# Projections as a stream of row-tile pairs, one-chunk score visits and AV by two pairs of heads, in a fused attention and feed-forward kernel

## Chip, cores, metric

One core of one Trainium2 chip. The metric is the device time of one execution in microseconds (us), the median of several runs. The clock granted to TensorE was full (1.00, or 0.99 over a whole run) throughout. A span from a profile is about 2 us shorter than the time of the same execution (466.3 against 468.6); spans are compared with spans and times with times.

## The reference

```python
scores = q @ k.T / sqrt(64)                      # 8 batches, 12 heads, 448 tokens, head size 64
attn   = maximum(scores, 0) ** 2 / 448
x      = (attn @ v), heads side by side          # 3584 tokens x 768
xn     = x / sqrt(mean(x * x) + 1e-6) * rms_g
out    = (silu(xn @ w_gate) * (xn @ w_val)) @ w_out    # 768 -> 1536 -> 768
```

## The kernel before

The feed-forward of batch b runs on TensorE while the attention of batch b+1 is slipped in between as "units". Only batch 0's attention runs alone. `merge` spreads the units over the feed-forward's groups.

Three things matter here. First, the shape of the matmuls. Each projection is issued as two halves of 64 output columns (column tiles, 128x64), which run side by side in the array. The norm's sums have the same shape, and AV's tiles (112x64) are column tiles too. Scores have only 64 rows to contract (the head size) and run as two row tiles (64x128). Second, the PSUM: 3 banks for projections, 4 for scores, 1 for AV. Third, the order of visits: per pair of heads j, two score visits of two chunks each; the second is followed by AV of the pair before.

```python
    def scores(b, j, cs):                       # cs = (0, 1) or (2, 3)
        for c in cs:
            psS = ps_s.tile([P, 2, 512], FP32, name="psS", tag="psS")
            for hh in range(2):                 # two row tiles, 64x128
                nc.tensor.matmul(out=psS[:, hh, :S], lhsT=qkT[...][:, c * PC : c * PC + P], rhs=qkT[...], ...)
        ...                                     # relu on ACT or DVE, square on DVE one visit later
    def attend(b, j):                           # AV of one pair of heads: 8 matmuls 112x64
        psAV = ps_a.tile([P, S], FP32, name="psAV", tag="ps_a")
        ...
    def project(b, *groups):
        for kt in range(KT):
            for ps, (w_sb, fb) in zip(pss, groups):
                for h in range(0, P, D):        # two column tiles, 128x64
                    nc.tensor.matmul(out=ps[h : h + D, :], lhsT=w_sb[:, kt, fb * P + h : fb * P + h + D],
                                     rhs=xns[b][:, kt, :], start=(kt == 0), stop=(kt == KT - 1))
    def outproj(i, t, o, w):                    # w = 512, then 256
        ...                                     # same two column tiles, 12 steps
    def attention(b):
        for j in range(HP):
            add(0.5, lambda j=j: scores(b, j, (0, 1)))
            ...
            add(1.2, lambda j=j: scores(b, j, (2, 3)), lambda j=j: j and attend(b, j - 1))
        ...
```

## Time and profile before

| | before |
|---|---|
| time, median | 468.63 us |
| span of the profiled run | 466.3 us |
| TensorE (PE) busy | 97% |
| DVE, ACT busy | 61%, 54% |
| chain that ended last, share of PE | 91% |

The first lines are from the page of the profiled run of the kernel before: busy us, share of the span and instructions of each engine, then the chain of work that ended last.

```profile
PE 454.5 (97%) x4768; PEld 257.6 (55%) x4768; DVE 283.6 (61%) x449; ACT 252.5 (54%) x380; POOL 55.8 (12%) x48
...
PE 91%; DVE 3%; ACT 2%; DMA 1%; issue 1%; POOL 0%; ACTq 0%; DVEq 0%; POOLq 0%
```

So TensorE sets the time. But busy does not say full: the ends of matmuls are modelled and they overlap. The groups of PE's matmuls by form show shapes and the mean length of one (the figure after the comma, in ns):

```profile
L302 PE MATMUL psP<-xn,wv_sb 128*64 128x448 bf16 x1152 | 126.9, 353 | 0.3 <-ACT sil L312 0.3
...
L339 PE MATMUL psO<-wo_sb,hT 128*64 128x512 bf16 x672 | 77.5, 379 | 0.0
L201 PE MATMUL psS<-qkT 64*128 64x448 bf16 x384 | 54.0, 354 | 3.3 <-ACT r L215 2.6 <-DVE qkT L179 0.7
...
L339 PE MATMUL psO<-wo_sb,hT 128*64 128x256 bf16 x672 | 41.8, 273 | 0.0
```

`128*64` and `64*128` are the tiles: column tiles and row tiles. The last column is idle time just before the group. It is next to nothing but for 3.3 us before the scores, nearly all of it in batch 0's attention, which runs alone; so PE hardly waits for anybody. Where the time goes is only seen in the starts. The timeline of PE in one stretch (start us, length us, what, how many):

```profile
205.66 0.92 PE L302 MATMUL psP<-xn,wg_sb 128*64 128x448 bf16 x8
206.51 0.55 PE L201 MATMUL psS<-qkT 64*128 64x448 bf16 x4
207.00 1.32 PE L302 MATMUL psP<-xn,wv_sb 128*64 128x448 bf16 x12
208.15 1.30 PE L302 MATMUL psP<-xn,wg_sb 128*64 128x448 bf16 x12
```

From 207.00 to 208.15 one group of six pairs takes 1.15 us, or 189 ns a pair (its first pair is 24 ns longer). The score visit starts at 206.51 and ends at 207.00: 0.49 us for two pairs that take 0.38 in a stream. The single starts of the trace show the rest: 285 ns pass from the last projection pair to the first score pair and 279 to 283 ns from the last score pair back, where 189 would do. These are the changes between column and row tiles. The Trainium skill ("TensorEngine Tiling (Array Packing)", Key Properties) says that changing the tiling mode drains TensorE; the trace agrees, with about 95 ns each way.

### The profile page before, as it was taken

The numbers are of one execution on the slowest core, as the hardware profiler recorded it, in microseconds if no ns is written. First come the engines' busy times: TensorE is split into PE (matmuls) and PEld (weight loads), VectorE is DVE, ScalarE is ACT, GpSimd is POOL, SyncE is SP. The second block draws the span as 40 slices with busy tenths as digits, with TensorE's granted clock in tenths as the row PEclk, the third lists the DMA queues.
The fourth block names the chain that finished last, engine by engine and source line by source line (L and its number), as shares of the span: only waits on it lengthen the run. The fifth ranks groups of instructions, "written<-read, shape, count | busy, mean of one in ns | idle before, by whom it ended". The sixth has DMA issues, their size and how long they took to land.

```text
span 466.3 us, 10899 instructions
## 1 busy us (share of the span) xinstructions
PE 454.5 (97%) x4768; PEld 257.6 (55%) x4768; DVE 283.6 (61%) x449; ACT 252.5 (54%) x380; POOL 55.8 (12%) x48
## 2 busy tenths in 40 slices
PE   7989999999999999999999999999999999999995
PEld 3336654655456445655456554565456554577774
DVE  2876497757745677557665578457773677562210
ACT  4872476566545666546645666546665566452221
POOL 8463000421012000400004000000000000000000
PEclk9999999999999999999999999999999999999999
DMA  9999999999919920499009940086001300021013
GB/s 113 200 204 200 209 168 129 116 208 158 82 33 173 201 29 1 53 214 135 1 2 143 211 83 1 7 173 103 1 2 38 100 2 1 0 70 34 1 37 101
DMA packets 128047, 43.56 MB, mean 93 GB/s; under 512 B 100608, under 2 KB 124416, under 8 KB 128000
## 3 DMA queue, kind: packets, MB, share of 16 engines
q0 software_dynamic: 88944, 23.60, 52.0%
q1 hardware_dynamic: 39056, 19.28, 20.9%
q8 instruction: 37, 0.61, 0.5%
q14 instruction: 10, 0.08, 0.1%
HBM read 47.19 MB, written 11.01 MB: 125 GB/s over the span
## 4 chain that ended last, share of the span: by engine, by line
PE 91%; DVE 3%; ACT 2%; DMA 1%; issue 1%; POOL 0%; ACTq 0%; DVEq 0%; POOLq 0%
PE psP L302 48%; PE psO L339 23%; PE psS L201 9%; PE psAV L230 8%; DVE r L218 2%; PE psB L139 1%; PE psSS L276 1%; DMA kb<-in_k_dram 1%; ACT r L215 1%; DVE r L213 1%; PE psT L174 1%; ACT xT L241 1%; DVE x L243 0%; POOL qb L93 0%; POOL kb L93 0%
## 5 line engine op out<-in xcount | busy, mean ns | idle before, releaser
L215 ACT ACTIVATE r<-psS 112x896 bf16<-112x896 f32 x147 | 128.4, 915 | 28.6 <-PE psS L201 28.4
L302 PE MATMUL psP<-xn,wv_sb 128*64 128x448 bf16 x1152 | 126.9, 353 | 0.3 <-ACT sil L312 0.3
L302 PE MATMUL psP<-xn,wg_sb 128*64 128x448 bf16 x1152 | 126.8, 353 | 0.0
L339 PE MATMUL psO<-wo_sb,hT 128*64 128x512 bf16 (+1 forms) x1344 | 112.5, 326 | 0.0
L317 DVE TENSOR_TENSOR hT<-sil,psP 128x448 bf16<-128x448 bf16 x96 | 59.6, 621 | 84.7 <-PE psP L302 82.6
L218 DVE TENSOR_TENSOR r<-r 112x896 bf16<-112x896 bf16 x189 | 109.9, 626 | 0.2 <-ACT r L215 0.2
L312 ACT ACTIVATE sil<-psP 128x448 bf16<-128x448 f32 x96 | 52.2, 545 | 97.2 <-PE psP L302 97.1
L339 PEld LDWEIGHTS <-hT 128*64 128x64 bf16 x1344 | 78.9, 110 | 31.7 <-issue 0.4
L302 PEld LDWEIGHTS <-wg_sb 128*64 128x64 bf16 x1152 | 66.4, 110 | 45.4 <-issue 7.4
L302 PEld LDWEIGHTS <-wv_sb 128*64 128x64 bf16 x1152 | 65.5, 110 | 46.7 <-issue 10.5
L346 ACT COPY ost<-psO 128x512 f32<-128x512 f32 (+1 forms) x56 | 26.7, 478 | 73.1 <-PE psO L339 73.1
L213 DVE TENSOR_SCALAR r<-psS 112x896 bf16<-112x896 f32 x45 | 49.0, 1089 | 27.6 <-PE psS L201 27.6
L201 PE MATMUL psS<-qkT 64*128 64x448 bf16 x384 | 54.0, 354 | 3.3 <-ACT r L215 2.6
L230 PE MATMUL psAV<-r,vb 112*64 112x448 bf16 x384 | 46.1, 358 | 1.0 <-DVE r L218 1.0
L285 DVE RECIPROCAL rstd<-rstd 128x448 f32<-128x448 f32 x8 | 23.6, 2953 | 19.9 <-ACT rstd L281 19.9
L201 PEld LDWEIGHTS <-qkT 64*128 64x128 bf16 x384 | 11.9, 94 | 37.7 <-issue 33.1
L230 PEld LDWEIGHTS <-vb 112*64 112x64 bf16 x384 | 18.4, 109 | 24.0 <-issue 15.3
L243 DVE TENSOR_TENSOR x<-xT 128x448 bf16<-128x448 bf16 x48 | 18.5, 385 | 20.7 <-ACT xT L241 20.7
L241 ACT ACTIVATE xT<-psAV 128x448 bf16<-128x448 f32 x48 | 26.2, 545 | 8.2 <-PE psAV L230 6.6
L93 POOL DMA_DIRECT2D vb<-in_v_dram x9 | 8.7, 970 | 178.7 <-PE psAV L230 177.5
L288 DVE SCALAR_TENSOR_TENSOR xn<-xT,g_sb,rstd 128x448 bf16<-128x448 bf16 x48 | 29.3, 680 | 0.3
L95 POOL DMA_DIRECT2D qb<-in_q_dram x6 | 13.8, 2299 | 43.7 <-DMA qkT<-qb 38.1
(29 smaller groups left out, 126.3 us busy)
## 6 DMA issues: line engine op xcount, KB each, us to landing
qb<-in_q_dram POOLq DMA_DIRECT2D x7, 672.0 KB, 13.4
kb<-in_k_dram POOLq DMA_DIRECT2D x7, 672.0 KB, 19.9
vb<-in_v_dram POOLq DMA_DIRECT2D x7, 672.0 KB, 8.2
out_dram<-ost SPq DMA_DIRECT2D x8, 336.0 KB, 3.7
wg_sb<-in_moe_w_gate_dram POOLq DMA_DIRECT2D x4, 576.0 KB, 18.0
wv_sb<-in_moe_w_val_dram POOLq DMA_DIRECT2D x4, 576.0 KB, 19.7
wo_sb<-in_moe_w_out_dram POOLq DMA_DIRECT2D x2, 1152.0 KB, 26.2
out_dram<-ost SPq DMA_DIRECT2D x8, 288.0 KB, 4.6
```

Source lines behind the costliest of these rows:

```text
L201: nc.tensor.matmul(out=psS[:, hh, :S], lhsT=qkT[b][prt, j].rearrange("p t s -> p (t s)")[:, c * PC : c * PC + P], rhs=qkT[b][prt, j, 1, :] ...
L213: nc.vector.tensor_relu(out=r[:], in_=psS[:PC, :, :S])
L215: nc.scalar.activation(out=r[:], in_=psS[:PC, :, :S], func=ACT.Relu)
L218: lambda r=r, eng=eng: eng.tensor_tensor(out=r[:], in0=r[:], in1=r[:], op=ALU.mult)
L230: nc.tensor.matmul(out=psAV[hh * D : (hh + 1) * D, :], lhsT=ld["v", b][:, 2 * j + hh, c * D : (c + 1) * D], rhs=rsq[b, j, c][:, hh, :], st ...
L241: nc.scalar.mul(out=xT[:, j, :], in_=psAV[:], mul=inv_attn)
L288: nc.vector.scalar_tensor_tensor(out=xn[:, kt, :], in0=xTs[b][:, kt, :], scalar=g_sb[:, kt : kt + 1], in1=rstd[:], op0=ALU.mult, op1=ALU.mult,
L302: nc.tensor.matmul(out=ps[h : h + D, :], lhsT=w_sb[:, kt, fb * P + h : fb * P + h + D], rhs=xns[b][:, kt, :], start=(kt == 0), stop=(kt == ...
L312: nc.scalar.activation(out=s[:], in_=psG[:], func=ACT.Silu)
L317: nc.vector.tensor_tensor(out=hTs[b // 2][:, fb, o : o + S], in0=sil[b, fb][:], in1=psV[:], op=ALU.mult)
L339: nc.tensor.matmul(out=ps[h : h + D, :w], lhsT=hTs[i][:, fk, t * P + h : t * P + h + D], rhs=wo_sb[:, fk, o : o + w], start=(fk == 0), sto ...
L346: nc.scalar.copy(out=ost[:, o : o + w], in_=ps[:, :w])
```

## The change

Its intent: put scores, projections and sums into one mode. Everything but AV becomes row tiles of 64x128 (the transposes of batches 0 and 1, batch 0's sums and its first three projections stay column tiles too). The two row tiles of one product would add into the same PSUM bank, and the kernel keeps them from doing so at once: the halves work on different groups. The lead half does rows 0 to 63 of a group, and the other half follows on the same bank seven pairs later. Before a half takes a group over, the last matmul of the other half must have ended; a `nop` with a semaphore carries that wait.

Output tiles are cut into three pieces of 256 columns in rotation, each in two visits of six pairs. AV now handles two pairs of heads at a time, in three visits per batch, and takes its PSUM from the scores' buffers. Scores come one chunk per visit. Besides, the norm's product xn has one buffer in place of two; this costs no wait that the trace shows, as PE has none over 150 ns after 41 us.

```diff
-    ps_a = ... bufs=1
-    ps_m = ... bufs=3
+    ps_m = ... bufs=4
-    def scores(b, j, cs):            # two chunks
+    def scores(b, j, c):             # one chunk
     def attend(b, j):
-        psAV = ps_a.tile([P, S], FP32, name="psAV", tag="ps_a")
+        psAV = ps_s.tile([P, 2, 512], FP32, name="psAV", tag="psS")
+        for jj in range(2):          # two pairs of heads
     def attention(b):
         for j in range(HP):
-            add(0.5, lambda j=j: scores(b, j, (0, 1)))
-            add(1.2, lambda j=j: scores(b, j, (2, 3)), lambda j=j: j and attend(b, j - 1))
+            for c in range(NCH):
+                if c == 1 and j in (2, 4):
+                    add(1.6, lambda j=j: attend(b, j - 2))
+                add(0.3, lambda j=j, c=c: scores(b, j, c))
+                ...                  # batch 0 and 1: transposes, fillers
+    class Stream:
+        APART = 2                    # pairs of rest before the other half may take a group
+        ...
+        def step(self):
+            ...
+            lead = self.pick(0, None)
+            follow = self.pick(1, lead)
+            for half, g in ((0, lead), (1, follow)):
+                if g is not None:
+                    g.emit(half)
+            ...
+    class Group:
+        ...
+        def emit(self, half):
+            i = self.count[half]
+            prt = slice(half * D, (half + 1) * D)
+            if self.last not in (None, half):
+                tc.add_manual_dep(nc.tensor.nop().ins, self.mm.name, behind)
+            mm = nc.tensor.matmul(out=self.ps[:, : self.w], lhsT=self.lhsT(i)[prt], rhs=self.rhs(i)[prt],
+                start=(half == 0 and i == 0), stop=(half == 1 and i == self.n - 1))
+            ...
+    def norm_sums(b):                # the sums are a group of the stream
+        return Group(KT, S, lambda i: ones_bf[:], lambda i: x2s[b][:, i, :], ..., "psSS")
+    OW = DM // 3                     # three pieces in rotation
...
-        for fn in merge(main, side, 0.3 if b == 0 else 0.0, 0.18):
+        for g in groups:
+            for _ in range(g.n):
+                while k < len(side) and done >= total * (head + (1 - head - tail) * k / len(side)):
+                    side[k][1]()
+                    k += 1
+                stream.step()
+                ...                  # count what is done
```

More of the change, by code (lines that the diff above doesn't have):

```diff
@@ L15 @@
 NCH = 4
-def merge(main, side, head=0.0, tail=0.0):
-    total = sum(c for c, _ in main)
-    if not main:
-        return [f for _, f in side]
-    out, done, k = [], 0.0, 0
-    n = len(side)
-    for c, f in main:
-        while k < n and done >= total * (head + (1.0 - head - tail) * k / n):
-            out.append(side[k][1])
-            k += 1
-        out.append(f)
-        done += c
-    out.extend(f for _, f in side[k:])
-    return out
 @with_exitstack
@@ L67 @@
     qtpool = ctx.enter_context(tc.tile_pool(name="qkT", bufs=2))
-    apool = ctx.enter_context(tc.tile_pool(name="attn", bufs=10))
+    apool = ctx.enter_context(tc.tile_pool(name="attn", bufs=12))
     xpool = ctx.enter_context(tc.tile_pool(name="xT", bufs=1))
@@ L74 @@
     ps_s = ctx.enter_context(tc.tile_pool(name="ps_s", bufs=2, space=bass.MemoryType.PSUM))
-    ps_a = ctx.enter_context(tc.tile_pool(name="ps_a", bufs=1, space=bass.MemoryType.PSUM))
-    ps_m = ctx.enter_context(tc.tile_pool(name="ps_m", bufs=3, space=bass.MemoryType.PSUM))
+    ps_m = ctx.enter_context(tc.tile_pool(name="ps_m", bufs=4, space=bass.MemoryType.PSUM))
     ld = {}
@@ L192, in flush @@
             pending.pop(0)()
-    def scores(b, j, cs):
-        pss = []
-        for c in cs:
-            psS = ps_s.tile([P, 2, 512], FP32, name="psS", tag="psS")
-            for hh in range(2):
-                prt = slice(hh * D, (hh + 1) * D)
-                nc.tensor.matmul(
-                    out=psS[:, hh, :S],
-                    lhsT=qkT[b][prt, j].rearrange("p t s -> p (t s)")[:, c * PC : c * PC + P],
-                    rhs=qkT[b][prt, j, 1, :],
-                    start=True,
-                    stop=True,
-                )
-            pss.append(psS)
-        squares = []
-        for c, psS in zip(cs, pss):
-            r = apool.tile([PC, 2, S], BF16, name="r", tag="r")
-            if relu_on(b, j, c) == "dve":
-                nc.vector.tensor_relu(out=r[:], in_=psS[:PC, :, :S])
-            else:
-                nc.scalar.activation(out=r[:], in_=psS[:PC, :, :S], func=ACT.Relu)
-            eng = nc.gpsimd if square_on(b, j, c) == "pool" else nc.vector
-            squares.append(
-                lambda r=r, eng=eng: eng.tensor_tensor(out=r[:], in0=r[:], in1=r[:], op=ALU.mult)
-            )
-            rsq[b, j, c] = r
+    def scores(b, j, c):
+        psS = ps_s.tile([P, 2, 512], FP32, name="psS", tag="psS")
+        for hh in range(2):
+            prt = slice(hh * D, (hh + 1) * D)
+            nc.tensor.matmul(
+                out=psS[:, hh, :S],
+                lhsT=qkT[b][prt, j].rearrange("p t s -> p (t s)")[:, c * PC : c * PC + P],
+                rhs=qkT[b][prt, j, 1, :],
+                start=True,
+                stop=True,
+            )
+        r = apool.tile([PC, 2, S], BF16, name="r", tag="r")
+        if relu_on(b, j, c) == "dve":
+            nc.vector.tensor_relu(out=r[:], in_=psS[:PC, :, :S])
+        else:
+            nc.scalar.activation(out=r[:], in_=psS[:PC, :, :S], func=ACT.Relu)
+        eng = nc.gpsimd if square_on(b, j, c) == "pool" else nc.vector
@@ L221, in scores @@
         flush()
-        pending.extend(squares)
+        pending.append(lambda: eng.tensor_tensor(out=r[:], in0=r[:], in1=r[:], op=ALU.mult))
+        rsq[b, j, c] = r
     x2s = {}
     def attend(b, j):
-        psAV = ps_a.tile([P, S], FP32, name="psAV", tag="ps_a")
-        for c in range(NCH):
-            for hh in range(2):
-                nc.tensor.matmul(
-                    out=psAV[hh * D : (hh + 1) * D, :],
-                    lhsT=ld["v", b][:, 2 * j + hh, c * D : (c + 1) * D],
-                    rhs=rsq[b, j, c][:, hh, :],
-                    start=(c == 0),
-                    stop=(c == NCH - 1),
-                )
+        psAV = ps_s.tile([P, 2, 512], FP32, name="psAV", tag="psS")
@@ L237, in attend @@
+        for jj in range(2):
+            for c in range(NCH):
+                for hh in range(2):
+                    nc.tensor.matmul(
+                        out=psAV[hh * D : (hh + 1) * D, jj, :S],
+                        lhsT=ld["v", b][:, 2 * (j + jj) + hh, c * D : (c + 1) * D],
+                        rhs=rsq[b, j + jj, c][:, hh, :],
+                        start=(c == 0),
+                        stop=(c == NCH - 1),
+                    )
         if j == 0:
@@ L239, in attend @@
             x2s[b] = npool.tile([P, KT, S], BF16, name="x2", tag="x2", bufs=1)
-        xT = xTs[b]
-        nc.scalar.mul(out=xT[:, j, :], in_=psAV[:], mul=inv_attn)
+        xT = xTs[b][:, j : j + 2, :]
+        nc.scalar.mul(out=xT, in_=psAV[:, :, :S], mul=inv_attn)
         pending.append(
-            lambda: nc.vector.tensor_tensor(
-                out=x2s[b][:, j, :], in0=xT[:, j, :], in1=xT[:, j, :], op=ALU.mult
-            )
+            lambda: nc.vector.tensor_tensor(out=x2s[b][:, j : j + 2, :], in0=xT, in1=xT, op=ALU.mult)
         )
@@ L256, in attention @@
         for j in range(HP):
-            add(0.5, lambda j=j: scores(b, j, (0, 1)))
-            if b < PE_T and j + 1 < HP:
-                add(0.4, lambda j=j: transposes(b, j + 1))
-            if b == 0:
-                add(0.3, lambda: keep_busy(2))
-            add(1.2, lambda j=j: scores(b, j, (2, 3)), lambda j=j: j and attend(b, j - 1))
-            if b == 0:
-                add(0.3, lambda: keep_busy(2))
+            for c in range(NCH):
+                if c == 1 and j in (2, 4):
+                    add(1.6, lambda j=j: attend(b, j - 2))
+                add(0.3, lambda j=j, c=c: scores(b, j, c))
+                if c == 1 and b < PE_T and j + 1 < HP:
+                    add(0.4, lambda j=j: transposes(b, j + 1))
+                if b == 0 and c % 2:
+                    add(0.3, lambda: keep_busy(2))
@@ L265, in attention, with __init__, add, first @@
         add(0.1, flush)
-        add(0.8, lambda: attend(b, HP - 1), flush)
+        add(1.6, lambda: attend(b, HP - 2), flush)
         return units
     xns, hTs = {}, {}
+    class Stream:
+        APART = 2
+        def __init__(self):
+            self.todo, self.open, self.at = [], [], [None, None]
+        def add(self, groups):
+            self.todo += groups
+        def first(self, groups):
+            self.todo[:0] = groups
+        def pick(self, half, taken):
+            here = self.at[half]
+            order = ([here] if here in self.open and here.count[half] % KT else []) + self.open
+            for g in order:
+                if g is not taken and g.ready(half):
+                    return g
+            if half == 0 and self.todo:
+                g = self.todo.pop(0)
+                self.open.append(g)
+                g.begin()
+                return g
+            return None
+        def step(self):
+            if not (self.todo or self.open):
+                return False
+            lead = self.pick(0, None)
[3 more added lines that the diff above has]
+                    g.emit(half)
+            self.at = [lead, follow]
+            for g in self.open:
+                g.rest += 1
+            if follow is not None and follow.count[1] == follow.n:
+                self.open.remove(follow)
+                follow.done(follow.ps)
+            return True
+        def run(self):
+            while self.step():
+                pass
@@ new lines, with __init__, bound, ready @@
+    stream = Stream()
+    behind = mybir.DependencyInfo(mybir.DependencyClass.Sync, mybir.DependencyReason.DATA)
+    class Group:
+        handed = 0
+        def __init__(self, n, w, lhsT, rhs, done, name):
+            self.n, self.w, self.lhsT, self.rhs, self.done, self.name = n, w, lhsT, rhs, done, name
+            self.count, self.rest, self.last = [0, 0], 0, None
+        def bound(self):
+            return self.n
+        def ready(self, half):
+            if self.last not in (None, half) and self.rest < stream.APART:
+                return False
+            return self.count[half] < (self.count[0] if half else self.bound())
+        def begin(self):
+            self.ps = ps_m.tile([P, 512], FP32, name=self.name, tag="mm")
+        def emit(self, half):
[3 more added lines that the diff above has]
+                tc.add_manual_dep(nc.tensor.nop().ins, self.mm.name, behind)
+            mm = nc.tensor.matmul(
+                out=self.ps[:, : self.w], lhsT=self.lhsT(i)[prt], rhs=self.rhs(i)[prt],
+                start=(half == 0 and i == 0), stop=(half == 1 and i == self.n - 1),
+            )
+            self.count[half] += 1
+            self.last, self.rest = half, 0
+            self.mm = mm.ins
@@ new lines, with __init__, bound @@
+    class Piece(Group):
+        def __init__(self, trio, *args):
+            super().__init__(*args)
+            self.trio = trio
+            trio.append(self)
+        def bound(self):
+            h = self.n // 2
+            if self.count[0] >= h and any(g.count[0] < h for g in self.trio):
+                return h
+            return self.n
+    def norm_sums(b):
+        return Group(
+            KT, S, lambda i: ones_bf[:], lambda i: x2s[b][:, i, :],
+            lambda ps: norm_scale(b, ps), "psSS",
+        )
@@ L272, in norm @@
     def norm(b):
-        psSS = ps_m.tile([P, S], FP32, name="psSS", tag="mm")
+        psSS = ps_m.tile([P, 512], FP32, name="psSS", tag="mm")
         for kt in range(KT):
@@ L276, in norm, with norm_scale @@
                 nc.tensor.matmul(
-                    out=psSS[h : h + D, :], lhsT=ones_bf[:, h : h + D], rhs=x2s[b][:, kt, :],
+                    out=psSS[h : h + D, :S], lhsT=ones_bf[:, h : h + D], rhs=x2s[b][:, kt, :],
                     start=(kt == 0), stop=(kt == KT - 1),
                 )
+        norm_scale(b, psSS)
+    def norm_scale(b, psSS):
         rstd = npool.tile([P, S], FP32, name="rstd", tag="rstd", bufs=1)
         nc.scalar.activation(
-            out=rstd[:], in_=psSS[:], func=ACT.Sqrt, scale=1.0 / float(DM), bias=eps_col[:]
+            out=rstd[:], in_=psSS[:, :S], func=ACT.Sqrt, scale=1.0 / float(DM), bias=eps_col[:]
         )
@@ L285, in norm @@
         nc.vector.reciprocal(out=rstd[:], in_=rstd[:])
-        xn = npool.tile([P, KT, S], BF16, name="xn", tag="xn")
+        xn = npool.tile([P, KT, S], BF16, name="xn", tag="xn", bufs=1)
         for kt in range(KT):
@@ L319, in hidden, with projection @@
         )
-    def gate(b, fb):
-        silu(b, fb, *project(b, (wg_sb, fb)))
-    def value(b, fb):
-        hidden(b, fb, *project(b, (wv_sb, fb)))
+    def projection(b, w_sb, fb, then):
+        return Group(
+            KT, S, lambda i: w_sb[:, i, fb * P : (fb + 1) * P], lambda i: xns[b][:, i, :],
+            lambda ps: then(b, fb, ps[:, :S]), "psP",
+        )
     def gate_value_gate(b):
@@ L333, with outproj, store @@
     osts = {}
-    def outproj(i, t, o, w):
-        ps = ps_m.tile([P, 512], FP32, name="psO", tag="mm")
-        for fk in range(FT):
-            for h in range(0, P, D):
-                nc.tensor.matmul(
-                    out=ps[h : h + D, :w], lhsT=hTs[i][:, fk, t * P + h : t * P + h + D],
-                    rhs=wo_sb[:, fk, o : o + w], start=(fk == 0), stop=(fk == FT - 1),
-                )
-        if o == 0:
-            osts[i, t] = opool.tile([P, DM], FP32, name="ost", tag="ost")
-        ost = osts[i, t]
+    OW = DM // 3
+    def outproj(i, t):
+        trio = []
+        for o in range(0, DM, OW):
+            Piece(
+                trio, FT, OW, lambda fk: hTs[i][:, fk, t * P : (t + 1) * P],
+                lambda fk, o=o: wo_sb[:, fk, o : o + OW],
+                lambda ps, o=o: store(i, t, o, OW, ps), "psO",
+            )
+        return trio
+    def store(i, t, o, w, ps):
+        if (i, t) not in osts:
+            osts[i, t] = [opool.tile([P, DM], FP32, name="ost", tag="ost"), 0]
+        ost = osts[i, t][0]
         nc.scalar.copy(out=ost[:, o : o + w], in_=ps[:, :w])
-        if o + w == DM:
+        osts[i, t][1] += w
+        if osts[i, t][1] == DM:
             g, end = t * P, (t + 1) * P
@@ L358, in ffn @@
     def ffn(b):
-        units = []
-        if b == 0:
-            units.append((3.4, lambda: gate_value_gate(b)))
+        groups = []
         for fb in range(FT):
             if b or fb > 1:
-                units.append((1.13, lambda fb=fb: gate(b, fb)))
+                groups.append(projection(b, wg_sb, fb, silu))
             if b or fb:
-                units.append((1.13, lambda fb=fb: value(b, fb)))
+                groups.append(projection(b, wv_sb, fb, hidden))
         full = S // P
         for t in range(full) if b % 2 == 0 else range(full, NT):
-            units.append((2.56, lambda t=t: outproj(b // 2, t, 0, 512)))
-            units.append((1.28, lambda t=t: outproj(b // 2, t, 512, DM - 512)))
-        return units
+            groups += outproj(b // 2, t)
+        return groups
     keep_busy(16)
-    for fn in merge([], attention(0) + [(1.1, lambda: norm(0))]):
+    for _, fn in attention(0) + [(1.1, lambda: norm(0))]:
         fn()
@@ L383 @@
         if b + 1 < B:
-            side = attention(b + 1) + [(1.1, lambda b=b: norm(b + 1))]
-        main = ffn(b)
+            side = attention(b + 1) + [(0.0, lambda b=b: stream.first([norm_sums(b + 1)]))]
+        if b == 0:
+            gate_value_gate(b)
+        groups = ffn(b)
+        slots = sum(g.n for g in groups)
+        stream.add(groups)
+        head, tail = 0.25 if b == 0 else 0.0, 0.18
         if b + 2 < B:
@@ L388 @@
                 load(nm, b + 2)
-            at = len(main) * 2 // 3
-            main[at:at] = [(0, lambda b=b: transpose_dma(b + 2))]
-        for fn in merge(main, side, 0.3 if b == 0 else 0.0, 0.18):
+            side.insert(len(side) * 2 // 3, (0, lambda b=b: transpose_dma(b + 2)))
+        cost = {KT: S / 2.4 + 2.5, FT: OW / 2.4 + 2.5}
+        total = sum(g.n * cost[g.n] for g in groups)
+        done, k = 0.0, 0
+        for g in groups:
[4 more added lines that the diff above has]
+                stream.step()
+                done += cost[g.n]
+        for _, fn in side[k:]:
             fn()
+    stream.run()
 _INS = ['q', 'k', 'v', 'moe_w_gate', 'moe_w_val', 'moe_w_out', 'moe_rms_g']
```

## The prediction

> **What bounds it now.** TensorE. The page's busy table gives PE 97% (454.5 of 466.3 us), ACT 54%, DVE 61%; the chain that ended last is 91% PE; the waits of PE sum to about 6 us. Busy overstates use, so I counted starts in the timeline. Two 128x64 column halves run together: a pair of 448-wide projection matmuls starts every 189 ns, a 512-wide output pair every 215 ns, a 256-wide one every 108 ns. That is already the streaming rate; the change cannot speed up a pair.
>
> What is lost is mode changes. A score visit runs 64x128 row tiles, all else 128x64 column tiles. The timeline shows 285 ns from the last projection pair to the first score pair and 279-283 ns back, against 189: about 95 ns each way, and the first pair after a change is 11 ns (row) or 24 ns (column) longer, because its weights were not preloaded. The Trainium skill, "TensorEngine Tiling (Array Packing)", Key Properties, says that a change of tiling mode drains the array; the trace agrees, at about 95 ns. Twelve visits per batch cost 12 x 0.22 = 2.6 us. From 95 to 418 us (six batches) the span exceeds the sum of the pairs by 17 us, of which 13 are the changes themselves.
>
> **Removed.** Scores, projections and sums now share the row mode: seven overlapped batches x 2.6 = about 18 us.
>
> **Added.** (1) AV stays in column mode: three visits per batch, each two changes plus the skew between the halves, about 0.29 us: 6 us over seven batches. (2) Batch 1's six transpose visits now change mode too: 1.7 us. Net of these: -10 us. (3) A handover nop: the second half may touch a group only after the first half's last matmul has ended. A 448-wide row matmul takes 349 ns, and consumers in the trace start about 40 ns after an end, against two pairs (378 ns): absorbed by a skew of some 50 ns, free. A 256-wide one takes about 270 ns, so 310 plus issue and weight load, about 350, against two or at most three pairs (215-323 ns): an estimated 20-45 ns lost at each of 168 handovers (28 tiles x 3 pieces x 2), 3-7 us. (4) Norm: its sums enter the stream later (79% of a batch's slots instead of 76%) and take 13 pairs (about 2.4 us) instead of 1.25. Before, the last norm product (xn) landed only 1.4 (first batch) to 2.5 us before its use; I expect 1-2 us of stall at the first transitions, less later, in all 2-3 us; single-buffered xn costs nothing as projections end well before. (5) Drain of the lag, and a longer last AV before the first norm: 1.5 us. Output pieces 3x256 instead of 512+256 stream equally (323 ns per k-step); ACT gains 0.15 us per tile, off the path. One-chunk visits smooth ACT and DVE.
>
> **Sum.** -18 + 6 + 2 + 5 + 2.5 + 1.5 = about -1; but lag and rotation look chosen to avoid (3), so I shade to -3 us: **465.5 us**, 80% range 456 to 475. Chances: faster by over 2% 0.22, within 2% 0.63, slower 0.15.
>
> **What would show it.** Projection and score pairs at 189 ns without a 285 ns gap around scores; gaps only round AV (and batch 1 transposes); output pieces at 108 ns per pair plus a kink every six; at each new batch's first gate group, PE waiting for DVE's xn.
>
> **What would make it wrong.** Row pairs slower than 189 ns in a long stream (only two in a row are seen before); the nop costing far more, by starving weight preload (449 handovers x 100 ns would be 45 us: slower); or handovers and norm being free (about -8 to -10 us: faster by 2%).

## The result and the profile after

| | before | after |
|---|---|---|
| time, median | 468.63 us | 468.94 us |
| ratio | | 1.0006, 95% interval 0.9992 to 1.0020 |
| span of the profiled run | 466.3 us | 467.2 us |
| PE busy | 97% | 97% |
| DVE, ACT busy | 61%, 54% | 61%, 55% |

A ratio is the mean time of one kernel's fast runs over that of the other's in the same rounds, so it is not quite the ratio of the medians that are quoted. Nothing was gained: I had forecast a gain of 3 us, and there is none.

The page of after, its busy line and the chain:

```profile
PE 455.1 (97%) x5440; PEld 297.1 (64%) x5440; DVE 283.0 (61%) x425; ACT 255.6 (55%) x384; POOL 55.7 (12%) x48
...
PE 92%; DVE 4%; ACT 3%; issue 0%; DVEq 0%
```

PE still sets the time. The groups by form, as before (all stream matmuls are now one line of the program, 317):

```profile
L317 PE MATMUL psP<-xn,wv_sb 64*128 64x448 bf16 x1140 | 236.1, 349 | 0.0
...
L317 PE MATMUL psO<-wo_sb,hT 64*128 64x256 bf16 x2016 | 141.2, 270 | 0.0
L179 PE MATMUL psS<-qkT 64*128 64x448 bf16 x384 | 77.7, 350 | 3.8 <-ACT r L190 3.0 <-DVE qkT L160 0.7
```

The shapes are all row tiles, and again nobody makes PE wait: the 3.8 us before the scores lie before the first projection, and after 41 us the list of PE's waits is empty. The busy time of psP nearly doubled while the run got no longer: the two halves no longer start together, and overlaps of different groups are counted in each. It is a warning against reading such busy times as cost. The timeline of PE around a score visit:

```profile
207.13 0.35 PE L317 MATMUL psP<-xn,wv_sb 64*128 64x448 bf16 x1
207.17 0.69 PE L317 MATMUL psP<-xn,wg_sb 64*128 64x448 bf16 x3
207.54 0.36 PE L317 MATMUL psP<-xn,wv_sb 64*128 64x448 bf16 x1
207.70 0.39 PE L179 MATMUL psS<-qkT 64*128 64x448 bf16 x2
207.89 0.35 PE L317 MATMUL psP<-xn,wg_sb 64*128 64x448 bf16 x1
207.93 0.35 PE L317 MATMUL psP<-xn,wv_sb 64*128 64x448 bf16 x1
```

The score pair starts at 207.70 and the next lead pair at 207.89: 189 ns, as in the stream. The gaps around scores are gone, and row pairs run at the same 189 ns as column pairs. In the 108 stretches of six or more projection pairs between 97 and 416 us the excess over 189 ns a pair was 0.6 us in all (0.2 on the lead half, 1.0 on the other), so the handovers of 448-wide groups are next to free. So far the mechanism is what I had predicted. The gain must have been given back elsewhere, and three places show it.

**Output pieces.** The starts of one pure output stretch of after in the trace (ns from one lead start to the next; each is followed by its partner 3 to 4 ns later):

```
109 109 109 109 119 120   109 109 109 109 120 119   ...
```

Every six pairs, at the handover, two pairs lose about 10 ns each, 21 in all: the wait of the weight load ends so late that weights are no longer loaded ahead (at 198.31 the load starts 4 ns before its matmul, the next ones 108 ns before theirs). Over 168 such handovers (28 token tiles, three pieces, twice each) this would be 3.5 us. But only about 120 of them show the loss; the rest fall beside score visits or sums. The gaps of this kind sum to 2.4 us on either half.

**Unequal widths.** The timeline of PE at the norm's sums of batch 3, which are 448 wide among pieces 256 wide:

```profile
195.83 0.36 PE L317 MATMUL psSS<-x,ones_bf 64*128 64x448 bf16 x1
195.83 0.39 PE L317 MATMUL psO<-wo_sb,hT 64*128 64x256 bf16 x2
196.03 0.35 PE L317 MATMUL psSS<-x,ones_bf 64*128 64x448 bf16 x1
196.06 0.38 PE L317 MATMUL psO<-wo_sb,hT 64*128 64x256 bf16 x2
196.22 0.35 PE L317 MATMUL psSS<-x,ones_bf 64*128 64x448 bf16 x1
196.28 0.38 PE L317 MATMUL psO<-wo_sb,hT 64*128 64x256 bf16 x2
196.40 0.73 PE L317 MATMUL psSS<-x,ones_bf 64*128 64x448 bf16 x3
196.82 0.53 PE L317 MATMUL psO<-wo_sb,hT 64*128 64x256 bf16 x5
```

One half runs the sums at 189 ns, the other its pieces at 109 ns. The faster one runs ahead, and then stands still from 196.39 (its last start) to 196.82: it is held by the next weight load with a semaphore wait, which belongs to the slower half and lets nothing pass. I count an idle half as half a pair lost. I worked out the excess of such stretches as their length minus their pairs at 189 ns (448 wide) and 109 ns (256 wide). Each of the seven sums costs about 0.41 us (the last 0.24), 2.7 us in all; the entries into the output phase cost 2.1 us and the exits 1.1, as there one half is still on projections and the other on pieces. That is 5.9 us, of which handovers, a wait for xn at the first border and one AV visit that falls into such a stretch make some 0.8. About 5 us remain.

**The start.** The timelines of before and of after at the first projection:

```profile
38.61 0.38 PE L302 MATMUL psP<-xn,wg_sb 128*64 128x448 bf16 x2
```

```profile
40.64 0.38 PE L378 MATMUL psP<-xn,wg_sb 128*64 128x448 bf16 x2
```

It starts at 40.6 us in after and at 38.6 in before. I had sized what is added there, together with the drain of the lag, at 1.5 us.

### The profile page after: what moved, and what is told of

It is laid out like the page before. It is cut to its first block, busy times and chain, and to the rows that moved or that the text cites. A ratio compares the mean times of both kernels' runs of the same rounds, so it can differ in the third digit from the quotient of the medians.

```text
span 467.2 us, 12220 instructions
## 1 busy us (share of the span) xinstructions
PE 455.1 (97%) x5440; PEld 297.1 (64%) x5440; DVE 283.0 (61%) x425; ACT 255.6 (55%) x384; POOL 55.7 (12%) x48
## 4 chain that ended last, share of the span: by engine, by line
PE 92%; DVE 4%; ACT 3%; issue 0%; DVEq 0%
PE psP L317 47%; PE psO L317 23%; PE psAV L203 8%; PE psS L179 7%; PE psB L120 2%; PE psSS L317 2%; ACT r L190 2%; DVE r L188 1%; PE psT L155 1%; DVE r L193 1%; DVE xn L364 1%; PE psP L378 1%; DVE rstd L361 1%; ACT xT L214 0%; DVE qkT L160 0%
## 5 line engine op out<-in xcount | busy, mean ns | idle before, releaser
L317 PE MATMUL psP<-xn,wv_sb 64*128 64x448 bf16 x1140 | 236.1, 349 | 0.0
L317 PE MATMUL psP<-xn,wg_sb 64*128 64x448 bf16 x1128 | 234.1, 349 | 0.1
L317 PE MATMUL psO<-wo_sb,hT 64*128 64x256 bf16 x2016 | 141.2, 270 | 0.0
L317 PEld LDWEIGHTS <-hT 64*128 64x128 bf16 x2016 | 103.3, 94 | 30.3 <-issue 3.1
L317 PEld LDWEIGHTS <-wv_sb 64*128 64x128 bf16 x1140 | 94.9, 94 | 41.5 <-issue 2.7
L317 PEld LDWEIGHTS <-wg_sb 64*128 64x128 bf16 x1128 | 94.5, 94 | 38.5 <-issue 3.2
L179 PE MATMUL psS<-qkT 64*128 64x448 bf16 x384 | 77.7, 350 | 3.8 <-ACT r L190 3.0
L427 ACT COPY ost<-psO 128x256 f32<-128x256 f32 x84 | 30.8, 372 | 42.9 <-PE psO L317 38.8
L214 ACT ACTIVATE xT<-psAV 128x896 bf16<-128x896 f32 x24 | 22.0, 917 | 41.4 <-PE psAV L203 40.2
L179 PEld LDWEIGHTS <-qkT 64*128 64x128 bf16 x384 | 26.5, 94 | 18.5 <-issue 11.0
L216 DVE TENSOR_TENSOR x<-xT 128x896 bf16<-128x896 bf16 x24 | 14.9, 622 | 23.6 <-ACT xT L214 23.6
```

What stands on the lines that cost most here:

```text
L179: nc.tensor.matmul(out=psS[:, hh, :S], lhsT=qkT[b][prt, j].rearrange("p t s -> p (t s)")[:, c * PC : c * PC + P], rhs=qkT[b][prt, j, 1, :] ...
L214: nc.scalar.mul(out=xT, in_=psAV[:, :, :S], mul=inv_attn)
L317: mm = nc.tensor.matmul(out=self.ps[:, : self.w], lhsT=self.lhsT(i)[prt], rhs=self.rhs(i)[prt], start=(half == 0 and i == 0), stop=(half = ...
L427: nc.scalar.copy(out=ost[:, o : o + w], in_=ps[:, :w])
```

## The experiments

All kernels below gave the right result. Times are medians in us; the kernel before was 468.3 to 468.7 in the same rounds. The 95% intervals of the ratios reach at most 0.003 to each side; by a rule of 2% only av_one_pair and mode_back differ from before, so smaller effects rest on these intervals and on the traces.

| run | what | us | ratio to before |
|---|---|---|---|
| after | | 468.94 | 1.0006 |
| av_one_pair | AV in six visits, batches 1 to 7 | 480.95 | 1.0269 |
| av_one_later | the same, one chunk later | 477.24 | 1.0185 |
| mode_back | mode changes back at score visits | 489.97 | 1.0459 |
| apart3 | one more pair of rest | 466.06 | 0.9949 |
| out384 | pieces 384 wide | 468.96 | 0.9999 |
| paced | sums run at once, attention ends earlier | 470.61 | 1.0041 |
| out384_paced | out384 and paced | 474.16 | 1.0117 |
| now | paced, sums ahead of pieces in rotation | 476.49 | 1.0164 |
| out384_now | out384 and now | 464.11 | 0.9900 |
| norm_column | sums outside the stream | 474.47 | 1.0128 |
| paced_sums224 | paced, sums as 2 x 224 | 472.26 | 1.0076 |
| start_old | batch 0's attention as before | 467.31 | 0.9985 |
| start_av | batch 0's AV by one pair | 467.79 | 0.9989 |
| start_apart3 | start_old and apart3 | 464.49 | 0.9910 |
| best_d | out384_now and start_old | 462.76 | 0.9871 |
| best_f | best_d, attention ends a little later | 462.27 | 0.9882 |
| best_g | best_f and apart3 | 462.41 | 0.9867 |

My theory: the removed mode changes were worth what I had counted, and the sum was eaten by AV's own changes, handovers, unequal widths and the start. Rivals: the removed changes were never worth 18 us; or waits for the norm's product xn, my term of 2 to 3 us, hold the gain.

### Were the mode changes worth it? mode_back, av_one_pair, av_one_later

The first run adds, ahead of two of the four score pairs of each j, a matmul of 16 columns in column mode whose result is not used:

```diff
         psS = ps_s.tile([P, 2, 512], FP32, name="psS", tag="psS")
+        if b and c % 2 == 0:
+            nc.tensor.matmul(out=psS[:D, 0, S : S + 16], lhsT=ones_bf[:, :D], rhs=busy_bf[:, :16],
+                             start=True, stop=True)
```

> After's kernel with a 16-wide column-tile matmul (its result is not used) ahead of the first and third score pair of every j in batches 1 to 7: 84 visits again change the mode twice, as in the kernel before. Theory A (the change really removed about 18 us of mode changes, and other things gave it back): 84 x (0.22 to 0.36 us, the second figure from av_one_later) + 84 x 0.02 = +20 to +32 us, 489 to 501. Rival (the removed mode changes were worth little, which is why nothing was gained): under +10 us.

Measured: 489.97, +21.0 us for 84 visits, or 0.25 us each. The timeline of PE in mode_back at one of them:

```profile
124.62 0.35 PE L322 MATMUL psP<-xn,wg_sb 64*128 64x448 bf16 x1
124.66 0.35 PE L322 MATMUL psP<-xn,wv_sb 64*128 64x448 bf16 x1
124.94 0.20 PE L178 MATMUL psS<-busy_bf,ones_bf 128*64 128x16 bf16 x1
125.07 0.36 PE L184 MATMUL psS<-qkT 64*128 64x448 bf16 x2
```

From the last projection (124.66) to the dummy 280 ns pass, and 129 more to the scores, for which 16 columns need next to nothing. With some 0.02 us taken off for each dummy, about 19 us are mode changes, with what the halves lose at each drain (they start 40 ns apart before it and together after it). So the largest term of my sum, 18 us, is right, and the rival that doubted it falls.

The next two give batches 1 to 7 twice as many AV visits, each of one pair of heads:

```diff
-                if c == 1 and j in (2, 4):
-                    add(1.6, lambda j=j: attend(b, j - 2))
+                if b and c == 1 and j:             # av_one_later: c == 2
+                    add(0.8, lambda j=j: attend_one(b, j - 1, ps_s, "psS"))
```

> After's kernel with AV in six visits of one pair of heads per batch (batches 1 to 7) in place of three of two: the number of mode changes for AV doubles, all other work is the same. Theory A (each mode change costs about 95 ns plus a longer first pair, on the path of PE): 21 more visits x 0.22 to 0.29 us = +4.6 to +6.1 us over after's 468.9, so about 474, ratio to before 1.010 to 1.014. Rival (mode changes are hidden or were never the loss, and that is why after gained nothing): below +1.5 us.

Measured: 480.95, +12.0, twice what I expected. The trace gives 5.0 us more at the borders of the visits, as expected, and 4.7 us more inside them, five of the six large ones in batch 1: AV came before its last squares were done.

> av_one_pair cost 12 us, of which its trace shows 5.0 at the borders of AV visits (mode changes) and 4.7 inside them, waiting for squares. Here the same visits come one chunk later, so that the squares are done. Theory A: the waits go and the mode changes stay, +5 us over after, about 474, ratio 1.011. Rival (the 12 us are the price of a visit as such): ratio 1.025 again.

Measured: 477.24, +8.3. The waits inside the visits are down to 0.7 us over those of after. So a visit costs up to 8.3 / 21 = 0.40 us in all, more than the 0.29 I had used. The gaps at its borders alone (90 ns in, 99 ns out, a first pair 24 ns longer) are 0.21. A count of the lost time of both halves in the traces (explained under "Why the prediction was right or wrong") separates the rest: at the AV visits themselves it rises from 5.2 us in after to 11.3 in av_one_later, 6.1 for 21 visits or 0.29 each, 0.7 of the 6.1 being waits for squares; the other 2.1 are lost at score visits (1.1), among output pieces and in projections. For the 21 visits of after the term is then 5.2 us, where I had 6.

### Handovers: apart3

```diff
-        APART = 2
+        APART = 3
```

> After's kernel with one more pair of rest before a half may take over a group (lag of eight pairs). Theory A (handovers of 256-wide pieces lose about 22 ns per six pairs in the trace of after, because the wait ends too late for the weights to be loaded ahead): the loss of 168 handovers, 3.7 us, goes, and one more pair of lag costs 0.7: -3 us, about 466, ratio to before 0.994. In the trace pure output stretches come to 109 ns a pair without the two 116 ns gaps per six. Rival (the loss belongs to the extra instruction or to row tiles as such): no gain, +0.7 us.

Measured: 466.06, -2.9 us, and in the trace the excess of pure output stretches has a median of 0 in place of 21 ns per six pairs: the steps from one lead start to the next (ns), from 197.18 us on, are

```
110 109 109 109 109 109   110 109 109 109 109 109   ...
```

The handover term is shown, but at less than I had: its gaps in the trace fall from 2.4 to 0.3 us, which is 2.1 of the 2.9. The other 0.8 us, and what the longer lag costs, are not separated.

### Unequal widths: out384 and its controls

Here the output is cut into 384-wide pieces, three of them (of two token tiles) in rotation. The fourth tile of odd batches keeps 3 x 256.

```diff
-        for o in range(0, DM, OW):
-            Piece(trio, FT, OW, ...)
+        cuts = [(t, o, DM // 2) for t in ts[:3] for o in range(0, DM, DM // 2)]
+        cuts += [(t, o, OW) for t in ts[3:] for o in range(0, DM, OW)]
+        for n, (t, o, w) in enumerate(cuts):
+            if n % 3 == 0:
+                trio = []
+            Piece(trio, FT, w, ...)
```

> After's kernel with output pieces 384 wide, three of them (from two token tiles) in rotation; the fourth tile of odd batches keeps 3 x 256. Theory A: (1) handovers become free, as a 384-wide pair leaves 2 x 162 ns plus a skew, -3.2 us; (2) steps that pair a 448-wide matmul of one half with a narrow one of the other lose 13 ns in place of 40 (about 26 such steps per batch: the sums 12, the two borders of the output phase 14), -4 to -5 us. Together -7 to -8 us: about 461, ratio to before 0.983. Rival B (only handovers cost): -3 us, ratio 0.994. Rival C (neither costs, the loss is waits for ACT and DVE): 0.

Measured: 468.96, nothing (its six runs spread from 466.7 to 469.8). But the trace showed that the stretches in question had become cheap (the sums 0.06 us each on average, against 0.38) and that two new waits ate it. The waits of PE in out384 between 400 and 414 us, and DVE's timeline there:

```profile
PE psO L317 <- DVE hT L393: 3.1, 1, 3.1
```

```profile
400.88 2.95 DVE L361 RECIPROCAL rstd<-rstd 128x448 f32<-128x448 f32 x1 [1.11 <-ACT rstd L357]
403.94 3.67 DVE L364 SCALAR_TENSOR_TENSOR xn<-xT,g_sb,rstd 128x448 bf16<-128x448 bf16 x6
407.52 0.61 DVE L393 TENSOR_TENSOR hT<-sil,psP 128x448 bf16<-128x448 bf16 x1
```

The sums are not counted among the slots of a batch, so the stream falls six steps further behind in each batch. In batch 6 the sums of batch 7 overtook the last projections of batch 6, and the last hidden product stood on DVE behind the whole norm. At the first border PE waited 1.9 us for xn. I mended the place of the sums, with a control that has the mended place and the old width:

```diff
+    def sums_now(b):
+        stream.first([norm_sums(b)])
+        for _ in range(KT):
+            stream.step()
...
-        head, tail = 0.25 if b == 0 else 0.0, 0.18
+        head, tail = 0.25 if b == 0 else 0.0, 0.22
```

> Control for the next run: after's kernel, where the six steps of the norm's sums are run at once when they enter the stream (no backlog grows from batch to batch) and the attention work ends a little earlier (0.22 of a batch before its end, not 0.18). Theory A: only the small xn stall at the first borders (about 0.3 us in the trace of after) is at stake: 468.5 +- 1, ratio 0.998 to 1.002. Rival (xn stalls of 2 to 3 us, as my prediction had them, are what cost after its gain): -2 to -3 us, ratio 0.994.

> out384 lost 3.1 us to one wait for hT at 404 us and 1.9 us to a wait for xn at 97 us, both because the sums came at the wrong place of the stream (the backlog); this run mends the place as in the run paced. Theory A (384-wide pieces save 3.2 us of handovers and 4.4 us of mixed widths): 461 to 463, ratio to before 0.984 to 0.988. Rival B (handovers alone): 465.5, ratio 0.994. Rival C (neither, the gain seen in the trace is paid elsewhere): as paced.

Measured: paced 470.61, +1.7 over after; out384_paced 474.16. The control fits that waits for xn did not hold the gain: with xn ready earlier the kernel got slower, not faster. (The trace of after says it directly: 0.3 us of such a wait, at the first border.) Of its 1.7 us the profiled runs show 1.1; by the count of lost time 0.8 more is lost at AV visits, 0.5 at handovers of pieces and 0.3 at sums and borders, and some 0.5 less elsewhere. Why AV's visits cost more there stays open. out384_paced failed for a reason of my own making: the sums may enter only when the lead half takes a new group, and it first finishes the pieces in rotation, up to 18 steps. They came so late that PE waited for xn at four borders, 11 us in all. So the next pair of runs lets the sums enter first:

```diff
         def pick(self, half, taken):
             here = self.at[half]
+            if (half == 0 and self.todo and self.todo[0].name == "psSS"
+                    and not (here in self.open and here.count[0] % KT)):
+                ...                  # begin the sums now
```

> Control for the next run, 256-wide pieces kept: the sums no longer wait for the pieces in rotation (up to 18 steps) before they enter the stream, six steps run at once, attention ends 0.22 to 0.25 of a batch early. Theory A (xn stalls were small in after): 469 to 471, ratio 1.000 to 1.005, like paced. Rival (waits for xn hold the gain): 466 or less.

> As the run now, with 384-wide pieces. out384_paced failed because the sums had to wait for the rotation (9.3 us of stalls at four borders in its trace), not because of the width. Theory A (widths nearer to each other and free handovers are worth 7 to 8 us): 462 to 463, i.e. 7 us under the run now, ratio to before 0.985. Rival B (handovers alone): 3 us under the run now. Rival C: equal to it. In the trace sums at about 80 ns of excess each against 413, output stretches with no 116 ns gaps.

Measured: now 476.49, out384_now 464.11. The control failed. The waits of PE in now after 43 us, and ACT's timeline at one of the borders:

```profile
PE psO L323 <- ACT ost L433: 3.8, 4, 0.9
```

```profile
198.09 1.28 ACT L363 ACT_TABLE_LOAD   x1
199.38 0.63 ACT L363 ACTIVATE rstd<-psSS,eps_col 128x448 f32<-128x448 f32 x1
200.03 1.28 ACT L131 ACT_TABLE_LOAD   x1
201.33 0.20 ACT L131 ACTIVATE scrap<-eps_col 128x1 f32<-128x1 f32 x1
201.44 0.63 ACT L433 COPY ost<-psO 128x256 f32<-128x256 f32 x2
```

With three pieces and the sums open, all four PSUM banks are taken, and while ACT spends 3.4 us on the root and its two table loads, it copies nothing out. The 256-wide pieces run out of banks; the 384-wide ones last long enough, and out384_now shows no such wait. Against now the difference is therefore too large as a verdict on widths (12.4 us). Against paced, which has no such wait but lets the sums in later, it is 6.5 us, near the 7 that I expected, and more than the 3.5 us that all handovers can give. In its trace six of the seven sums have an excess of 79 ns; one half then stays ahead and stands still later, so that to the point where the halves start together again it is about 0.25 us in four of the seven, against 0.51 in after (handovers included). The count of lost time divides the 5.4 us between the profiled runs of after and out384_now: 3.9 less at sums and borders, 1.9 less at handovers, 0.8 less because two 384-wide pieces take 325 ns a step and three 256-wide ones 328, 0.3 by the start, 0.3 less elsewhere, and 1.8 more at AV and score visits.

Two more runs tried to isolate the width of the sums. One takes them out of the stream, as a block in column mode:

```diff
-            side = attention(b + 1) + [(0.0, lambda b=b: stream.first([norm_sums(b + 1)]))]
+            side = attention(b + 1) + [(0.0, lambda b=b: norm(b + 1))]
```

> After's kernel with the norm's sums as one block of column-tile pairs outside the stream, as in the kernel before. Theory A (a 448-wide group among 256-wide ones costs 0.4 us, as in the trace of after: 12 steps at 189 ns while the other half idles): minus 0.4 and plus 0.22 for two mode changes, 7 times, so -1 us, and the sums take 1.3 us instead of 2.3. Rival (mixed widths cost nothing): +1.5 to +1.9 us.

The other splits them into two groups of 224 columns:

```diff
-        return Group(KT, S, lambda i: ones_bf[:], lambda i: x2s[b][:, i, :], ..., "psSS")
+        return [Group(KT, h, lambda i: ones_bf[:], lambda i, o=o: x2s[b][:, i, o : o + h], ..., "psSS")
+                for o in (0, h)]     # h = S // 2, one bank each, between two rotations of pieces
```

> The run paced (470.6) with the norm's sums as two groups of 224 columns in place of one of 448, which enter between two rotations of pieces. Theory A (a 448-wide group among 256-wide ones makes the other half idle, 413 ns of excess each in the trace of paced): excess about 160 ns plus one handover, -0.2 us each, 7 times, so -1.5 us: 469.1, ratio 1.001; trace: no 189 ns step among the output pieces. Rival (the width does not matter): 470.6 or, with 84 more matmul pairs' fixed cost, 471.

Measured: norm_column 474.47, paced_sums224 472.26. Both missed in time, and both by the wait just shown: PE waited 4.1 us for ACT's copies in the first, 2.5 us for ACT in the second (there the two sums hold two banks; its profiled run was 3 us above its median, with the first projection at 43.8 us, so only its local figures are used). In place, the effect was as expected: the excess at the sums fell from 413 to 217 ns in norm_column (what is left is two mode changes) and to 177 ns in paced_sums224. So the local cost of unequal widths is shown in three kernels, each time near the expected size; that the whole time falls with it is shown only by out384_now, in which the freed handovers take part.

### The start: start_old, start_av

start_old gives batch 0, and it alone, the attention of before: visits of two chunks and AV by one pair, with psAV in the bank pool of the projections. start_av only undoes the AV:

```diff
-                if c == 1 and j in (2, 4):
+                if b == 0 and c == 3 and j:
+                    add(0.8, lambda j=j: attend_one(b, j - 1, ps_m, "mm"))
+                if b and c == 1 and j in (2, 4):
                     add(1.6, lambda j=j: attend(b, j - 2))
```

> After's kernel with the attention of batch 0, which runs before any projection, as in the kernel before (two-chunk visits, AV by one pair). Theory A (the first projection starts 2.0 us later in after, 40.6 against 38.6 us, because nothing overlaps this stage and its last AV, copy, square and sums are longer): -2.0 us, about 467, ratio to before 0.997, the first projection at 38.6 us again. Rival (the later start is made up afterwards by waits that go): 0.

> After's kernel with AV by one pair of heads in batch 0 only, score visits stay by one chunk. Theory A (the last AV, copy, square of a double pair make the norm late): most of the 1.6 us of start_old, so -1.2 us, 467.7. Rival (the one-chunk visits, more mode changes between fillers and scores): 0.

Measured: 467.31 (-1.6) and 467.79 (-1.15). So the double AV makes most of it. Nothing overlaps batch 0's attention, and its tail is a chain: in after the last copy and square take 0.92 and 0.62 us for two pairs, in before 0.54 and 0.39 for one. The interval of start_old (0.9966 to 1.0003) is wide because one of its six runs, the profiled one, was 3 us longer with a later arrival of the first inputs; its profile is not used. That the first projection would start at 38.6 us again is not shown: in start_apart3, with the same start, it does so at 39.3, in start_av at 39.5.

### Together: start_apart3, best_d, best_f, best_g

These put parts that were tested above together; best_f only changes best_d's tail from 0.22 to 0.20 (batch 0: 0.25 to 0.24).

> After's kernel with both single gains, the old start (-1.6) and three pairs of rest (-2.9): if they are independent parts of the sum, -4.5 us: 464.4, ratio 0.991. If they share a wait, less.

> out384_now with the old start: 1.6 us under out384_now, about 461, ratio 0.982 if theory A holds.

> best_d with the attention work ending 0.20 (batch 0: 0.24) of a batch early instead of 0.22 (0.25). If the denser attention work is what costs paced its 1.7 us: 462 or less; if not, 462.8 as best_d.

> best_f with three pairs of rest. Only the fourth token tile of odd batches has 256-wide pieces left (24 handovers x 22 ns = 0.5 us), the longer lag costs some 0.1: 461.8 against 462.3; if it is over 463, the longer lag hurts elsewhere.

Measured: 464.49, 462.76, 462.27 and 462.41. The first is the sum of its parts to 0.1 us (-4.45 against -1.6 and -2.9), so these two terms are independent. The last three do not differ beyond their spread; the guess that the denser attention work costs paced its 1.7 us got no support worth the name. They beat both kernels, by 1.2 to 1.3% against before.

## Why the prediction was right or wrong

The mechanism was right: PE bounds both kernels, the mode changes at score visits were 18 us, row pairs run at 189 ns, and AV, the transposes and the output handovers give about half of it back. The prediction was wrong in its final sum.

| term, us | predicted | shown by the runs |
|---|---|---|
| mode changes at score visits | -18 | -19 (mode_back); score visits still lose 1.6 in the trace |
| AV's 21 visits | +6 | +5.2 in the trace; 0.29 for each one added (av_one_later) |
| transposes of batch 1 | +1.7 | +1.3 (1.7 against 0.4 in the traces) |
| output handovers | +3 to +7, 5 in the sum | +2.4 in the trace; -2.9 when undone (apart3), 2.1 of it seen at the handovers |
| waits for xn | +2.5 | about 0.3 in the trace; paced gained nothing |
| unequal widths | not in the sum | about +5 in the trace; -3.9 in that of out384_now |
| 3 x 256 for 512 + 256 columns | 0 | +0.8 in the trace (328 against 325 ns a step) |
| start | within 1.5, with the drain of the lag | +2.0 in the trace; 1.6 undone by start_old, 1.15 of it the double AV |
| shading | -2 | 0 |

A count over the two traces closes the sum. For every matmul take the time from its start to the next start on its half, less what its width takes in a stream (189 ns for 448 columns, 215.5 for 512, 109.3 for 256), and average the two halves; which half a matmul of after belongs to follows from the order in which its program issues them.

| us | before | after |
|---|---|---|
| up to the first projection | 38.6 | 40.6 |
| all pairs at the pace of a stream | 400.7 | 401.5 |
| lost around scores and AV, waits there included | 18.5 | 6.8 (5.2 at AV) |
| lost around transposes | 0.4 | 1.7 |
| lost at handovers of output pieces | 0 | 2.4 |
| lost at sums and other unequal widths | 1.2 | 6.7 |
| lost among projections | 1.8 | 1.9 |
| one half idle at the end | 0 | 0.4 |
| sum, end of the last pair | 461.2 | 462.0 |

So 11.7 us went at scores and AV, within 0.3 of what I had counted for the two together (-18 and +6), and the other rows give all of it back. The rows are times at which PE lost, not tests of a cause; the causes are what the experiments tested.

The step that failed is the count of point (4) and of the sum: I took a step of the stream to cost the mean of its two halves whatever their widths. I did see that the sums would take 13 pairs, "about 2.4 us", instead of 1.25, and I counted this as a delay for the norm, not as 0.4 us of an idle half. The same holds at both borders of the output phase. In place of the xn stalls that I expected there, the runs showed this loss, of twice the size.

The second fault is the shading. The sum stood at -1, within 1.3 us of the result, by luck: the missing term was nearly made up by two that I had put too high (xn and the handovers). I then moved it to -3 because the lag "looked chosen to avoid" the handover loss. The trace shows that the loss is there. I had worked out 20 to 45 ns per handover from measured lengths, and it came to 21 at some 120 of the 168; a guess should not have outweighed that.

What stays open: why 21 more AV visits also cost 2.1 us away from the visits; why paced loses more at its AV visits; and a run that changes the widths alone and has no wait of its own.

## What to carry to other kernels

When a change takes out mode changes, ask what the new order pays for it in places that the old one did not have: here two halves that must be equally wide and must hand banks over, and a longer tail where nothing overlaps. When two tiles of the array work on different products, a step costs what the wider one needs if, as here, the next wait brings them together; choose piece widths near each other (384 beside 448 was better than 256) and keep pieces long enough for the handover wait. And before a control is trusted, look in its trace for a wait that it brings itself: five of these runs (out384, out384_paced, now, norm_column, paced_sums224) missed their expected time by a wait for DVE or ACT that was not what they tested.

## What the Trainium skill lacked or had wrong

- "TensorE: Matmul & The Clock Gate", section What overlaps and what doesn't, under Part 3, says that matmuls start and end strictly in program order. Between the two row tiles of after this did not hold for the starts (ends are modelled in a trace): lead and follower alternate in the program, yet output matmuls of one half started at 196.276 and 196.385 us, before the sums matmuls of the other half that started at 196.404 and 196.594 and stand ahead of both in the program. One half ran up to three steps ahead of the other, until the next weight load with a semaphore wait.
- "TensorEngine Tiling (Array Packing)", Key Properties, says that a mode change drains TensorE but gives no cost. Here it was about 95 ns each way between 128x64 and 64x128, with a first pair 11 or 24 ns longer; put back into after, a visit with two changes cost 0.25 us.
- The same page, Performance Considerations, says nothing of tiles with unequal widths. A 448-wide group of six steps among 256-wide ones cost 0.41 us of excess, 0.08 among 384-wide ones (0.51 and 0.25 when counted to the point where the halves start together again).
- The same page, Gotcha 1, says that row tiles may not use one bank at once and that software must synchronise. It gives no figure: at two pairs of distance the handover was next to free at 448 columns (0.6 us over 108 stretches) and cost 21 ns per six pairs at 256; with three pairs the median there was 0.
